# Reordering the head of a fused attention and gMLP kernel: q of the first block ahead of its k, loads in 128-row pieces, one store moved forward

## Chip, cores, metric

One core of one Trainium2 chip. The metric is device time in microseconds (us) of one execution. All runs in this document are at granted clock 0.997 to 1.0. The profiled span is about 1.7 us shorter than the time of the same execution.

## The reference, cut to what matters

```python
x  = A_x                                  # 1 x 2048 x 512, bf16
xn = layernorm(x)
# A: 32 heads of 16, a window of 8 keys two apart
q, k, v = split(xn @ wqkv);  o = softmax(q . k[gathered]) . v[gathered];  A = o @ wo
# B: gMLP
z = gelu(xn @ w_in);  z1, z2 = z[:, :688], layernorm(z[:, 688:])
B = (z1 * (w_sp @ z2 + b_sp)) @ w_out
return x + A + B
```

The change concerns the first 25 us only (normalise, transpose, q and k projections of the first two of four token blocks) and one store at the end.

## The kernel before: the parts that matter

A block is four tiles of 128 tokens. A tile is normalised on VectorE (`ln_stats`, `ln_apply`; the root on ScalarE), transposed into `xnT`, and multiplied with q's and k's weights on TensorE (PE). Block 0's tiles and the first two of block 1 are transposed on PE (`tr`) and copied out. All others go through a transposing DMA from SyncE (`tr_dma`). A call of `qk_part` with `m` 0 or 1 makes half of q, with 2 or 3 half of k; `b0, b1` are the tiles it covers.

```python
    def tr_dma(i):
        SP.dma_start_transpose(xnT[:, :, i * P:(i + 1) * P], xall[:, j, tb, :])
    ...
    load_wqk(SP, 0, 0, 2); load_wqk(SP, 0, 2, 4)       # q weights, 2 x 256 KB
    SP.dma_start(xall[:, 1, 0:2], xblk[1][:, 0:2])
    load_wqk(SP, 1)                                    # k weights, 512 KB
    ...
    warm_up(10)                    # PE work on a zero tile, 512 columns each
    ...
    for n in range(2, 4):
        ln_apply(i1[n])
        tr_dma(i1[n])              # tiles 2 and 3 of block 1: two transposing DMAs
    ...
    for c in range(3):
        qk_part(pqs[c], 1, c, 0, 2)        # block 1, first half
    pa3 = ps_aux.tile(...)
    qk_part(pa3, 1, 3, 0, 2)               # the `pa` group of the profile
    qk_copy(pa3, 1, 3, 0, 2)
    for c in range(3):
        qk_part(pqs[c], 1, c, 2, 4)        # block 1, second half: needs those two DMAs
        qk_copy(pqs[c], 1, c)
    ...
    for c in range(3): z matmuls ...       # "first z matmul" below (in the order list: z2.0)
```

Of the kernel before, what the change touches and what calls it, by code (L numbers as in the profile page):

```python
# [14 lines left out]
P = 128  # L15
S = 2048
D = 512
NT = S // P
TB = 4
TBS = 512  # L20
C = D // P
# [5 lines left out]
F = 1376  # L27
FH = 688
# [26 lines left out]
A35 A36 Oh0.1 Fe0.0 A37 Fe0.1 A38 G14 Fe0.2 Fe0.3 F0.2 F0.0 F0.1 s0.0 A39 s0.1 F0.3 A40 xr1 A41 Oh1.0 w13 A42  # L55
U10 Oh1.1 Fe1.0 U9 T8 Gi14 A43 Fe1.1 A44 T10 X13 A45 G11 s0.2 T9 A46 s0.3 F1.0 A47 A48 G13 F1.1 Gi11 s1.1 Xg13
U11 U12 Fe1.2 A49 T12 A50 A51 X14 A52 G15 Xg14 Fe1.3 U14 Gi13 F1.3 F1.2 A53 s1.2 T11 A54 T14 A55 O2 Gi15 s1.0
A56 U15 U13 T15 A57 Or2 xr2 Oh2.0 A58 A59 s1.3 Oh2.1 T13 Fe2.0 Fe2.1 xr3 F2.0 O3 Fe2.2 Fe2.3 F2.2 F2.1 s2.2
F2.3 s2.1 s2.3 Or3 Oh3.0 Oh3.1 F3.0 F3.1 s3.0 s3.1 s2.0 end
"""  # L60
NZ1 = 8
LASTCUT = 288
# [7 lines left out]
def kernel(  # L70
# [13 lines left out]
    V = nc.vector  # L84
    A = nc.scalar
    G = nc.gpsimd
    PE = nc.tensor
    SP = nc.sync
# [3 lines left out]
    xblk = x2.rearrange("(b j p) d -> j p b d", b=TB, j=4)  # L92
# [9 lines left out]
    xall = r_x[:, 0:4 * TB * D].rearrange("p (j b d) -> p j b d", j=4, b=TB)  # L102
    vp = r_x[:].rearrange("p (d t) -> p d t", d=DH)
    r_w = sb.tile([P, 8192], BF16, name="r_w")
    wqk = r_w[:, 0:4096].rearrange("p (s k f) -> p s k f", s=2, k=C)
# [30 lines left out]
    xnT = sb.tile([P, C, S], BF16, name="xnT")  # L136
    w_z2 = sb.tile([P, C, FH], BF16, name="w_z2")
# [27 lines left out]
    def load_x0(E, tb, h):  # L165
        E.dma_start(xall[:, 0, tb, 256 * h:256 * h + 256], x2[tb * TBS:tb * TBS + P, 256 * h:256 * h + 256])

    def load_wqk(E, s, k0=0, k1=C):
        E.dma_start(wqk[:, s, k0:k1],
                    A_wqkv[:, s * D:(s + 1) * D].rearrange("(k p) f -> p k f", p=P)[:, k0:k1])  # L170

    for tb in range(2):
        load_x0(SP, tb, 0)
        load_x0(A, tb, 1)
    for tb in range(2, TB):
        A.dma_start(xall[:, 0, tb], xblk[0][:, tb])
    load_wqk(SP, 0, 0, 2)
    load_wqk(SP, 0, 2, 4)
    SP.dma_start(xall[:, 1, 0:2], xblk[1][:, 0:2])
    load_wqk(SP, 1)  # L180
    SP.dma_start(xall[:, 1, 2:4], xblk[1][:, 2:4])
    for j in range(2, 4):
        SP.dma_start(xall[:, j], xblk[j])
    SP.dma_start(w_z2[:], B_w_in[:, FH:F].rearrange("(k p) f -> p k f", p=P))


    V.memset(warm[:, 0:P], 0.0)
# [17 lines left out]
    def ln_stats(i, parts=1):  # L205
        j, tb = i % 4, i // 4
        w = D // parts
        for h in range(parts):
            V.bn_stats(stats[:, i, 6 * h:6 * h + 6], xall[:, j, tb, w * h:w * h + w])  # L209
        V.bn_aggr(mv[:, i, :], stats[:, i, 0:6 * parts])  # L210

    def ln_root(sl):
        A.activation(rstd[:, sl], mv[:, sl, 1], ACT.Abs_reciprocal_sqrt, bias=eps_t[:])

    def ln_apply(i):
        j, tb = i % 4, i // 4
        V.tensor_scalar(xall[:, j, tb, :], xall[:, j, tb, :], mv[:, i, 0:1], rstd[:, i:i + 1],
                        ALU.subtract, ALU.mult)

    def tr(i):  # L220
        j, tb = i % 4, i // 4
        pt = ps_aux.tile([P, C, P], BF16, name="pt", tag="aux")
        for c in range(C):
            PE.transpose(pt[:, c, :], xall[:, j, tb, c * P:(c + 1) * P], ident[:])  # L224
        return pt

    def tr_copy(i, pt, c0=0, c1=C):
        A.copy(xnT[:, c0:c1, i * P:(i + 1) * P], pt[:, c0:c1, :])

    def tr_dma(i):  # L230
        j, tb = i % 4, i // 4
        SP.dma_start_transpose(xnT[:, :, i * P:(i + 1) * P], xall[:, j, tb, :])
# [57 lines left out]
    def qk_part(pq, j, m, b0, b1, ccs=(0, 1), p0=None, kcs=range(C)):  # L290
        sd, c0 = m // 2, 2 * (m % 2)
        p0 = b0 if p0 is None else p0
        xv = xnT[:].rearrange("p k (b j t) -> p k b j t", b=TB, j=4)
        for cc in ccs:
            for kc in kcs:
                PE.matmul(pq[:, cc, p0 * P:(p0 + b1 - b0) * P], wqk[:, sd, kc, c0 + cc:D:C],  # L296
                          xv[:, kc, b0:b1, j, :], start=(kc == 0), stop=(kc == C - 1))

    def qk_copy(pq, j, m, b0=0, b1=TB, p0=None):
        sd, c0 = m // 2, 2 * (m % 2)  # L300
        p0 = b0 if p0 is None else p0
        if sd == 0:
            dst = qs[:, j, c0:c0 + 2, b0 * P:b1 * P].rearrange("p c (b t) -> p c b t", b=b1 - b0)
        else:
            dst = ks[:, c0:c0 + 2, HALO:HALO + S].rearrange("p c (b j t) -> p c b j t", b=TB, j=4)[:, :, b0:b1, j, :]
        cast = A.copy(dst, pq[:, :, p0 * P:(p0 + b1 - b0) * P].rearrange("p c (b t) -> p c b t", b=b1 - b0))  # L306
        if sd == 1:
            for i in k_reads[j]:
                tc.declare_no_dep(cast.ins, i, reason="other token columns of the same rows")
            k_casts[j].append(cast.ins)  # L310

    def qk_tile():
        return ps_mm.tile([P, 2, TBS], F32, name="pq", tag="mm")
# [224 lines left out]
    def blk(j):  # L538
        return [4 * tb + j for tb in range(TB)]

    def col(i):
        return slice(i, i + 1)

    def blk_cols(j):
        return slice(j, NT, 4)
# [6 lines left out]
    t0, i1 = blk(0), blk(1)  # L552
    i2, i3 = blk(2), blk(3)
# [4 lines left out]
    for n in range(2):  # L558
        ln_apply(t0[n])
    tr_copy(t0[0], tr(t0[0]))  # L560
    pt1 = tr(t0[1])
    tr_copy(t0[1], pt1, 0, 2)
    tr_copy(t0[1], pt1, 2, 4)
    warm_up(1)
    warm_up(1, 2)
# [5 lines left out]
    pqs = [qk_tile() for _ in range(3)]  # L571
    qk_part(pqs[0], 0, 0, 0, 2, kcs=range(2))
    qk_part(pqs[0], 0, 0, 0, 2, kcs=range(2, 4))
    tr_copy(t0[2], tr(t0[2]))
    qk_part(pqs[1], 0, 1, 0, 2, (0,))
    tr_copy(t0[3], tr(t0[3]))
    qk_part(pqs[1], 0, 1, 0, 2, (1,))
    qk_part(pqs[2], 0, 2, 0, 2)
    for n in range(2):
        ln_stats(i1[n])  # L580
    ln_root(slice(1, 8, 4))
    ln_stats(i1[2])
    ln_apply(i1[0])
    ln_apply(i1[1])
    ln_stats(i1[3])
    for n in range(2):
        qk_part(pqs[n], 0, n, 2, 4)
        qk_copy(pqs[n], 0, n)
    ln_root(slice(9, 16, 4))
    ln_stats(i2[0])  # L590
    for n in range(2, 4):
        ln_apply(i1[n])
        tr_dma(i1[n])
    qk_part(pqs[2], 0, 2, 2, 4, (0,))
    tr_copy(i1[0], tr(i1[0]))
    qk_part(pqs[2], 0, 2, 2, 4, (1,))
    tr_copy(i1[1], tr(i1[1]))
    qk_copy(pqs[2], 0, 2)
    pq3 = qk_tile()
    qk_part(pq3, 0, 3, 0, 4)  # L600
    qk_copy(pq3, 0, 3)
    for n in range(1, 4):
        ln_stats(i2[n])
    ln_root(blk_cols(2))
    ln_stats(i3[0])
    for i in i2:
        ln_apply(i)
        tr_dma(i)
    for n in range(1, 4):
        ln_stats(i3[n])  # L610
    pqs = [qk_tile() for _ in range(3)]
    for c in range(3):
# [76 lines left out]
```

## Time and profile before

| | before |
|---|---|
| time, median of the 6 runs beside the changed kernel | 203.12 us (202.78 to 203.41) |
| span of the profiled run | 201.6 us |
| PE's last matmul ends, last instruction to span end | 196.30, 5.3 us |
| first z matmul | 22.90 |

PE's timeline before, 18 to 23 us (start, length, what, count):

```profile
18.37 1.04 PE L296 MATMUL pa<-xnT,r_w 128*128 128x256 bf16 x8
19.25 3.66 PE L296 MATMUL pq<-xnT,r_w 128*128 128x256 bf16 x32
22.74 1.48 PE L238 MATMUL pz<-w_z,xnT 128*128 128x344 bf16 x9
```

The second line is block 1's second half. It follows the `pa` group without a bracket, that is without a wait. ("The chain" is the profile's list of the work that ended last, followed back piece by piece to what released it. The timeline puts a start about 0.16 us ahead of where the chain puts the same group when there is no wait: the chain has 18.54, 19.41 and 22.90.) Its input, the second transposing DMA's result, had come in time. SyncE's part of it, and a view of these DMAs with the time from issue to landing, in the kernel before:

```profile
14.63 10.39 SPq L232 DMA_TRANSPOSE xnT<-r_x  x7
DMA to landing us min/median/max: 2.4/2.5/3.0
```

The second one was issued at 16.04; its last packet was done by 17.99 (table below) and it landed at 18.44, so there was about 1 us of slack to 19.41.

### The profile page before, as it was taken

How to read it: one execution, taken by the hardware profiler on the slowest of the kernel's cores; microseconds unless marked ns; L12 is line 12 of the kernel's file. 1: busy time of each engine (PE TensorE's matmuls, PEld its weight loads, DVE VectorE, ACT ScalarE, POOL GpSimd, SP SyncE). 2: the span in 40 equal slices, each digit the busy share in tenths (PEclk: the TensorE clock that was granted, in tenths of full speed). 3: DMA queues.
4: the chain of work that ended last, by engine and by line, in shares of the span. 5: the costliest groups of instructions: out<-in, count | busy, mean ns of one | idle time of the engine just before them, and what ended most of it. 6: DMA issues, size and time to landing. Idle time of an engine off the chain costs nothing.

```text
span 201.6 us, 4025 instructions
## 1 busy us (share of the span) xinstructions
PE 196.2 (97%) x1667; PEld 124.7 (62%) x1667; DVE 184.4 (91%) x247; ACT 103.7 (51%) x172; POOL 18.3 (9%) x14
## 2 busy tenths in 40 slices
PE   7799999999999999999999999999999999999993
PEld 2589855665566666666656666666544646664562
DVE  5879699999989999999979999999999999999604
ACT  3565988899999996363341523808402230331400
POOL 3000000799500000000000000000000000000000
PEclk9999999999999999999999999999999999999999
DMA  5983549850000085544285999199920299215753
GB/s 151 337 279 74 90 98 273 177 111 0 3 0 3 0 134 109 162 92 104 62 150 135 247 255 166 34 227 169 224 65 0 87 222 142 73 42 129 205 177 130
DMA packets 66306, 25.91 MB, mean 129 GB/s; under 512 B 56240, under 2 KB 66032, under 8 KB 66032
## 3 DMA queue, kind: packets, MB, share of 16 engines
q1 hardware_dynamic: 65568, 25.19, 55.9%
q10 hardware_dynamic: 720, 0.47, 0.7%
q8 instruction: 13, 0.21, 0.4%
q14 instruction: 5, 0.04, 0.1%
HBM read 10.13 MB, written 2.10 MB: 61 GB/s over the span
## 4 chain that ended last, share of the span: by engine, by line
PE 92%; DMA 4%; DVE 1%; issue 0%; SPq 0%
PE pg L439 37%; PE pz L238 19%; PE pq L296 13%; PE pv L400 7%; PE po L522 7%; PE po L492 6%; DMA r_w<-in_A_wqkv_dram 3%; DMA r_x<-in_A_x_dram 1%; PE pa L522 1%; PE pl L350 1%; DVE r_pr L510 1%; PE po L501 1%; PE pb L492 1%; PE pa L296 0%; PE pt L224 0%
## 5 line engine op out<-in xcount | busy, mean ns | idle before, releaser
L439 PE MATMUL pg<-z,r_qk 128*128 128x344 bf16 x448 | 66.8, 309 | 0.0
L439 PEld LDWEIGHTS <-r_qk 128*128 128x128 bf16 x448 | 43.7, 98 | 22.0 <-issue 0.4
L414 DVE TENSOR_TENSOR r_pr<-r_x,r_w 128x2048 bf16<-128x2048 bf16 x32 | 38.4, 1219 | 1.3 <-PE pl L350 1.0
L238 PE MATMUL pz<-w_z,xnT 128*128 128x344 bf16 x256 | 39.3, 309 | 0.0
L418 DVE TENSOR_TENSOR r_pr<-r_pr 128x2048 bf16<-128x2048 bf16 x28 | 33.9, 1218 | 0.4
L238 PEld LDWEIGHTS <-xnT 128*128 128x128 bf16 x256 | 24.9, 98 | 13.2 <-issue 0.4
L445 ACT ACTIVATE gs<-pg,b_col 128x688 bf16<-128x688 f32 x16 | 13.2, 833 | 35.7 <-PE pg L439 26.4
L296 PE MATMUL pq<-xnT,r_w 128*128 128x256 bf16 (+1 forms) x176 | 28.7, 317 | 1.1 <-DMA r_w<-in_A_wqkv_dram 0.7
L330 DVE TENSOR_TENSOR r_pr<-r_qk 128x2048 bf16<-128x2048 bf16 x24 | 27.9, 1222 | 0.7 <-ACT r_qk L306 0.5
L296 PEld LDWEIGHTS <-r_w 128*128 128x128 bf16 x184 | 20.1, 114 | 8.8 <-issue 1.0
L631 POOL CAST b_col<-b 128x16 f32<-128x16 bf16 x1 | 16.2, 16244 | 34.1 <-DMA b<-in_B_b_sp_dram 34.1
L306 ACT CAST r_qk<-pq 128x1024 bf16<-128x1024 f32 (+1 forms) x16 | 15.4, 989 | 4.3 <-PE pq L296 4.1
L505 ACT CAST r_qk<-po 128x512 bf16<-128x512 f32 x10 | 5.5, 587 | 22.7 <-PE po L522 22.7
L287 ACT ACTIVATE r_uz<-pz 128x688 bf16<-128x688 f32 x16 | 11.7, 739 | 6.3 <-PE pz L238 6.2
L492 PE MATMUL po<-r_lg,r_pr 32*128 32x512 bf16 x192 | 14.5, 375 | 0.0
L400 PE MATMUL pv<-xnT,r_w 128*32 128x512 bf16 x256 | 14.2, 379 | 0.0
L522 PEld LDWEIGHTS <-r_uz 128*128 128x128 bf16 x85 | 8.0, 98 | 9.4 <-issue 1.1
L339 DVE TENSOR_TENSOR r_pr<-r_pr 128x4096 bf16<-128x4096 bf16 x6 | 13.7, 2288 | 0.0
L522 PE MATMUL po<-r_w,r_uz 128*128 128x512 bf16 x60 | 13.6, 380 | 0.0
L209 DVE BATCH_NORM_STATS2 stats<-r_x 128x6 f32<-128x512 bf16 (+1 forms) x18 | 10.9, 615 | 2.1 <-DMA r_x<-in_A_x_dram 2.1
L262 ACT ACTIVATE junk<-z 128x688 bf16<-128x688 bf16 x16 | 12.4, 773 | 0.1
L256 ACT ACTIVATE z<-pz 128x688 bf16<-128x688 f32 x16 | 11.8, 739 | 1.2 <-PE pz L238 1.2
(78 smaller groups left out, 184.6 us busy)
## 6 DMA issues: line engine op xcount, KB each, us to landing
r_lg<-in_A_wo_dram SPq DMA_DIRECT2D x8, 256.0 KB, 4.0
out_dram<-r_qk SPq DMA_DIRECT2D x12, 128.0 KB, 3.0
w_z<-in_B_w_in_dram SPq DMA_DIRECT2D x2, 688.0 KB, 6.8
r_w<-in_A_wqkv_dram SPq DMA_DIRECT2D x2, 512.0 KB, 5.3
r_x<-in_A_x_dram SPq DMA_DIRECT2D x2, 512.0 KB
r_qk<-in_A_x_dram SPq DMA_DIRECT2D x8, 128.0 KB, 2.5
r_w<-in_B_w_out_dram SPq DMA_DIRECT2D x1, 640.0 KB, 5.3
r_w<-in_A_wqkv_dram SPq DMA_DIRECT2D x2, 256.0 KB, 4.6
```

The costliest lines, as they stand in the source:

```text
L238: PE.matmul(pz[:, hh, 0:FHALF], xnT[:, kc, i * P:(i + 1) * P], wz[:, kc, hh * FHALF:(hh + 1) * FHALF], start=(kc == 0), stop=(kc == C - 1))
L296: PE.matmul(pq[:, cc, p0 * P:(p0 + b1 - b0) * P], wqk[:, sd, kc, c0 + cc:D:C], xv[:, kc, b0:b1, j, :], start=(kc == 0), stop=(kc == C - 1))
L306: cast = A.copy(dst, pq[:, :, p0 * P:(p0 + b1 - b0) * P].rearrange("p c (b t) -> p c b t", b=b1 - b0))
L330: prod = V.tensor_tensor(pr[g % 3][:, c].rearrange("p w b t -> p b w t"), q3.unsqueeze(2).broadcast_to([P, TB, 4, P]), k4, ALU.mult)
L339: V.tensor_tensor(pr[g % 3][:, 0:2], pr[g % 3][:, 0:2], pr[g % 3][:, 2:4], ALU.add)
L400: PE.matmul(pv[32 * tb:32 * tb + 32, dd, :], wv[:, kc, 2 * d2 + dd, :], xnT[:, kc, tb * TBS:(tb + 1) * TBS], start=(kc == 0), stop=(kc == ...
L414: V.tensor_tensor(pw_t[n], vp[:, :, off:off + P], a_sb[:, slot_w(w), ts].unsqueeze(1).broadcast_to([P, DH, P]), ALU.mult)
L418: V.tensor_tensor(pw_t[n] if dst is None else dst, pw_t[n], pw_t[m], ALU.add)
L439: PE.matmul(pg[:, hh, 0:FHALF], wsp[n][:, k, :], z2[:, k, hh * FHALF:(hh + 1) * FHALF], start=(k == 0), stop=(k == NT - 1))
L492: PE.matmul(pc, op[32 * tb:32 * tb + 32, d, o * P:(o + 1) * P], wo_r[32 * tb:32 * tb + 32, d, cs], start=(d == 8), stop=False, tile_positi ...
L522: PE.matmul(pc, uT[:, o % 2, m, tb * P:(tb + 1) * P], wout[:, m, cs], start=False, stop=(m == MCH - 3))
L631: G.tensor_copy(b_col[:], b16[:])
```

## The change

Intent: PE's wait for k's weights goes, because q of all four tiles of block 0 is done first; loads become 128 KB pieces in the order in which they are needed; roots are taken tile by tile so that normalisation does not wait for a pair; half of a PSUM copy moves to VectorE. The store that stood among the last ones is issued first of its group.

```diff
-F2.2 F2.1 s2.2 F2.3 s2.1 s2.3 ... s3.1 s2.0 end
+F2.2 F2.1 s2.0 s2.2 F2.3 s2.1 s2.3 ... s3.1 end
...
-    def load_wqk(E, s, k0=0, k1=C):
-        E.dma_start(wqk[:, s, k0:k1], ...)
+    def load_wqk(E, s):
+        for kc in range(C):
+            E.dma_start(wqk[:, s, kc], A_wqkv[kc * P:(kc + 1) * P, s * D:(s + 1) * D])
+    def load_x(E, j, b0, b1):            # one DMA of 128 rows per tile
...
-    for j in range(2, 4):
-        SP.dma_start(xall[:, j], xblk[j])
-    SP.dma_start(w_z2[:], ...)
+    load_x(SP, 2, 0, 4)
+    for kc in range(C):
+        SP.dma_start(w_z2[:, kc], ...)
...
+    def tr_copy_v(i, pt, c0, c1):        # the copy out of PSUM on VectorE
...
+    qk_part(pqs[1], 0, 1, 0, 2, (0,))
     tr_copy(t0[2], tr(t0[2]))
-    qk_part(pqs[1], 0, 1, 0, 2, (0,))
-    tr_copy(t0[3], tr(t0[3]))
-    qk_part(pqs[1], 0, 1, 0, 2, (1,))
-    qk_part(pqs[2], 0, 2, 0, 2)          # k, tiles 0 and 1: waits for k's weights
...
+    tr_copy_v(t0[3], pt3, 0, 2)
+    tr_copy(t0[3], pt3, 2, 4)
+    qk_part(pqs[0], 0, 0, 2, 4, kcs=range(2))    # q, tiles 2 and 3
+    qk_part(pqs[0], 0, 0, 2, 4, kcs=range(2, 4))
+    qk_part(pqs[1], 0, 1, 2, 4)
...
+    qk_part(pqs[2], 0, 2, 0, 4)          # k: 8 matmuls of 512 columns, were 16 of 256
...
     for n in range(2, 4):
         ln_apply(i1[n])
         tr_dma(i1[n])
+    load_x(SP, 3, 0, 4)                  # x of block 3 only here
```

More of the change, by code (lines that the diff above doesn't have):

```diff
@@ L57 @@
 U11 U12 Fe1.2 A49 T12 A50 A51 X14 A52 G15 Xg14 Fe1.3 U14 Gi13 F1.3 F1.2 A53 s1.2 T11 A54 T14 A55 O2 Gi15 s1.0
-A56 U15 U13 T15 A57 Or2 xr2 Oh2.0 A58 A59 s1.3 Oh2.1 T13 Fe2.0 Fe2.1 xr3 F2.0 O3 Fe2.2 Fe2.3 F2.2 F2.1 s2.2
-F2.3 s2.1 s2.3 Or3 Oh3.0 Oh3.1 F3.0 F3.1 s3.0 s3.1 s2.0 end
+A56 U15 U13 T15 A57 Or2 xr2 Oh2.0 A58 A59 s1.3 Oh2.1 T13 Fe2.0 Fe2.1 xr3 F2.0 O3 Fe2.2 Fe2.3 F2.2 F2.1 s2.0
+s2.2 F2.3 s2.1 s2.3 Or3 Oh3.0 Oh3.1 F3.0 F3.1 s3.0 s3.1 end
 """
@@ L166, in load_x0 @@
         E.dma_start(xall[:, 0, tb, 256 * h:256 * h + 256], x2[tb * TBS:tb * TBS + P, 256 * h:256 * h + 256])
-    def load_wqk(E, s, k0=0, k1=C):
-        E.dma_start(wqk[:, s, k0:k1],
-                    A_wqkv[:, s * D:(s + 1) * D].rearrange("(k p) f -> p k f", p=P)[:, k0:k1])
+    def load_wqk(E, s):
+        for kc in range(C):
+            E.dma_start(wqk[:, s, kc], A_wqkv[kc * P:(kc + 1) * P, s * D:(s + 1) * D])
+    def load_x(E, j, b0, b1):
+        for tb in range(b0, b1):
+            E.dma_start(xall[:, j, tb], xblk[j][:, tb])
     for tb in range(2):
@@ L174 @@
         load_x0(A, tb, 1)
-    for tb in range(2, TB):
-        A.dma_start(xall[:, 0, tb], xblk[0][:, tb])
-    load_wqk(SP, 0, 0, 2)
-    load_wqk(SP, 0, 2, 4)
-    SP.dma_start(xall[:, 1, 0:2], xblk[1][:, 0:2])
+    load_x(A, 0, 2, 4)
+    load_wqk(SP, 0)
+    load_x(SP, 1, 0, 2)
     load_wqk(SP, 1)
-    SP.dma_start(xall[:, 1, 2:4], xblk[1][:, 2:4])
-    for j in range(2, 4):
-        SP.dma_start(xall[:, j], xblk[j])
-    SP.dma_start(w_z2[:], B_w_in[:, FH:F].rearrange("(k p) f -> p k f", p=P))
+    load_x(SP, 1, 2, 4)
+    load_x(SP, 2, 0, 4)
+    for kc in range(C):
+        SP.dma_start(w_z2[:, kc], B_w_in[kc * P:(kc + 1) * P, FH:F])
     V.memset(warm[:, 0:P], 0.0)
@@ L228, in tr_copy @@
         A.copy(xnT[:, c0:c1, i * P:(i + 1) * P], pt[:, c0:c1, :])
+    def tr_copy_v(i, pt, c0, c1):
+        V.tensor_copy(xnT[:, c0:c1, i * P:(i + 1) * P], pt[:, c0:c1, :])
     def tr_dma(i):
@@ L573 @@
     qk_part(pqs[0], 0, 0, 0, 2, kcs=range(2, 4))
+    qk_part(pqs[1], 0, 1, 0, 2, (0,))
     tr_copy(t0[2], tr(t0[2]))
-    qk_part(pqs[1], 0, 1, 0, 2, (0,))
-    tr_copy(t0[3], tr(t0[3]))
-    qk_part(pqs[1], 0, 1, 0, 2, (1,))
-    qk_part(pqs[2], 0, 2, 0, 2)
-    for n in range(2):
-        ln_stats(i1[n])
-    ln_root(slice(1, 8, 4))
-    ln_stats(i1[2])
+    qk_part(pqs[1], 0, 1, 0, 2, (1,), kcs=range(2))
+    pt3 = tr(t0[3])
+    qk_part(pqs[1], 0, 1, 0, 2, (1,), kcs=range(2, 4))
+    tr_copy_v(t0[3], pt3, 0, 2)
[3 more added lines that the diff above has]
+    qk_part(pqs[1], 0, 1, 2, 4)
+    ln_stats(i1[0])
+    ln_root(col(i1[0]))
+    ln_stats(i1[1])
+    ln_root(col(i1[1]))
+    qk_copy(pqs[0], 0, 0)
     ln_apply(i1[0])
     ln_apply(i1[1])
-    ln_stats(i1[3])
-    for n in range(2):
-        qk_part(pqs[n], 0, n, 2, 4)
-        qk_copy(pqs[n], 0, n)
-    ln_root(slice(9, 16, 4))
-    ln_stats(i2[0])
+    qk_copy(pqs[1], 0, 1)
+    qk_part(pqs[2], 0, 2, 0, 4)
+    for n in range(2, 4):
+        ln_stats(i1[n])
+        ln_root(col(i1[n]))
     for n in range(2, 4):
@@ L593 @@
         tr_dma(i1[n])
-    qk_part(pqs[2], 0, 2, 2, 4, (0,))
+    load_x(SP, 3, 0, 4)
     tr_copy(i1[0], tr(i1[0]))
-    qk_part(pqs[2], 0, 2, 2, 4, (1,))
+    pq3 = qk_tile()
+    qk_part(pq3, 0, 3, 0, 4, (0,))
     tr_copy(i1[1], tr(i1[1]))
+    qk_part(pq3, 0, 3, 0, 4, (1,))
     qk_copy(pqs[2], 0, 2)
-    pq3 = qk_tile()
-    qk_part(pq3, 0, 3, 0, 4)
     qk_copy(pq3, 0, 3)
-    for n in range(1, 4):
+    for n in range(4):
         ln_stats(i2[n])
-    ln_root(blk_cols(2))
-    ln_stats(i3[0])
+    ln_root(slice(2, 7, 4))
+    ln_root(slice(10, 15, 4))
     for i in i2:
@@ L608 @@
         tr_dma(i)
-    for n in range(1, 4):
+    for n in range(4):
         ln_stats(i3[n])
```

## The prediction

> **What bounds the kernel now.** I read the page's first and fourth parts first. The second block is the chain of waits, in order of time, at its head.
>
> ```profile
> PE 196.2 (97%) x1667; PEld 124.7 (62%) x1667; DVE 184.4 (91%) x247; ACT 103.7 (51%) x172; POOL 18.3 (9%) x14
> PE 92%; DMA 4%; DVE 1%; issue 0%; SPq 0%
> ```
>
> ```profile
> 3.46 6.56 DMA r_w<-in_A_wqkv_dram
> 10.01 0.05 issue
> 10.06 3.25 PE pq L296 x28
> ```
>
> TensorE (PE) is busy for 97% of the span, but 97% is not the argument: the chain is. From 10.06 us the chain of the end consists of PE pieces only, without a break, until the last eviction at 196.3. The list of PE's waits from 22 us on is empty. So an instruction moved on another engine after 10.06 is worth something only if PE can be made to start its unbroken run earlier. What precedes that run is one transfer, the 512 KB of the k weights (issued at 3.46, landed 6.56 us later). The next view is PE's own timeline from 6 to 11 us (start, length, what, and in brackets the idle time before it):
>
> ```profile
> 6.74 1.03 PE L296 MATMUL pq<-xnT,r_w 128*128 128x256 bf16 x8 [0.40 <-ACT xnT L228]
> 7.91 0.40 PE L224 MATMUL pt<-ident,r_x 128*128 128x128 bf16 x4
> 8.14 0.60 PE L296 MATMUL pq<-xnT,r_w 128*128 128x256 bf16 x4
> 8.58 0.39 PE L224 MATMUL pt<-ident,r_x 128*128 128x128 bf16 x4
> 8.80 0.60 PE L296 MATMUL pq<-xnT,r_w 128*128 128x256 bf16 x4
> 10.06 3.25 PE L296 MATMUL pq<-xnT,r_w 128*128 128x256 bf16 x28 [0.65 <-DMA r_w<-in_A_wqkv_dram]
> ```
>
> The lengths overlap, so starts are what counts. Four matmuls of 256 columns need 4 x 0.109 = 0.44 us (later in the run, where PE never waits, 32 of them take 3.49 us in the chain, 0.109 each). Those that start at 8.80 have left the array's input free at 9.24, and the next starts at 10.06: a hole of 0.82 us, of which the view counts 0.65. What it waits for is k's weights; the q matmuls of the tiles 2 and 3, which need no k weights, stand behind it in program order.
>
> [...](3.49/32 = 0.109; eight of 512 columns in 1.73 us, 0.216 each). So turning 16 matmuls of 256 columns into 8 of 512 saves no PE time worth the name. [...]issues of 64, 128, 256 and 512 KB alike take 0.37 to 0.51 us here, and landing comes 2 to 6.6 us after. So cutting a load in four multiplies the issue time by four. [...]In the trace the engines move 341 to 357 GB/s from 7 to 14 us with the large loads; whether 128 KB loads reach that, nothing here shows yet.
>
> **The change part by part.**
>
> (a) *Order on PE.* The q matmuls of tiles 2 and 3 (16 of 256 columns, 1.74 us) move ahead of all k matmuls. Starting from 6.74: eight matmuls to 7.61, four to 8.05, the transposes of tile 2 (four, start to start 0.055 us) to 8.27, two matmuls to 8.49, transposes of tile 3 to 8.71, two matmuls to 8.93. The next group needs the transposed copies of tiles 2 and 3. ScalarE's copy of tile 2 starts at about 8.34 as before, 0.6 us, so 9.0; the new VectorE half copy of tile 3 starts at about 8.77 (its engine is free: the normalisation ends at 8.33) and takes some 0.3 us by estimate from ScalarE's 0.38 for a half; ScalarE's other half ends at 9.4. So PE goes on at about 9.2, with a hole of 0.25 in place of 0.82, and runs 16 matmuls to 10.93. k's weights are wanted at 10.93 (first quarter) to 11.6 (fourth) instead of 9.24. The state that PE had at 10.06 is reached at about 9.2: **0.86 us gained**.
>
> (b) *Loads of 128 KB.* The built order shows that each load waits for the one eight before it; that held before too, but with fewer, larger loads. Now k's weights are loads 13 to 16 and wait for x tiles and q weights that land at about 5 to 6.5. SyncE: 0.47 us each, the fourth quarter is issued at about 7 (before: whole at 3.46), and lands, with at most 1 MB outstanding at 340 GB/s (3 us), at 9.5 to 10. That is no earlier than the 10.01 of before, but PE now wants it at 11.6. So this wait should be gone with 1 to 2 us to spare. x of block 1, tiles 2 and 3, should land at 10 to 11 (before 10.80), wanted by VectorE at 11.5. Block 2 and the z weights follow by 13 to 15.5, wanted at 14.2 and 22. x of block 3 is issued only after the first transposing DMAs, at 16.3, lands by 20.5, wanted from 19.1 on, tile by tile.
>
> (c) *Roots tile by tile, and the rest of the head.* A pair's root becomes two of 0.29 us: 0.3 us more on ScalarE. VectorE: statistics and applications as before plus 0.3 for the copy. My schedule: statistics of block 1's first two tiles end at 10.75, applications at 11.5, next statistics at 13.1, applications at 14.2 (before 14.92). ScalarE: two q evictions at 11.05 to 13.0, roots to 13.5, transposed copies to 14.7, two k evictions to 16.7. PE finishes block 0 at 14.83 (before: 14.19 + 1.73 = 15.92) and block 1's third group waits about 0.15 for the eviction at 16.7; it starts the `pa` group at 17.6 against 18.54. So **0.9 us** is still there, and at the first z matmul (22.90 before, 22.0 now) too. VectorE starts its products 0.65 us earlier (24.0 instead of 24.69): its idle of 1.6 before the last normalisations shrinks.
>
> (d) *The store.* The tail in order of time:
>
> ```profile
> 198.03 0.42 SPq L517 DMA_DIRECT2D out_dram<-r_qk  x1
> 198.50 0.39 DVE L510 TENSOR_TENSOR r_pr<-pb,r_pr 128x224 bf16<-128x224 f32 x1
> 198.54 0.89 SPq L517 DMA_DIRECT2D out_dram<-r_pr  x2
> ```
>
> The store from r_qk at 198.03 is ready since about 191 and stands among the last ones. The final store can be issued when its addition ends at 198.89; it starts at 199.07, after its neighbour. Without the store between, the neighbour goes at 198.1 and the last at about 198.95: **0.1 us gained**. It costs 0.4 us of an idle queue earlier.
>
> The sum: 0.86 to 0.95 at the head, 0.1 at the end, about 1.0; I take 0.1 off for what is lost on the way. 203.12 - 0.9 = 202.2.
>
> **The rivals.**
> - *VectorE becomes the bound.* It is busy 91%, and gains only 0.65 in my schedule. The last additions of products end at 188.8 and PE reads them from 189.91: 1.1 us of slack; the second logits group at 48.7 comes 0.3 after its sums. If VectorE's gain rules, the total gain is 0.65 + 0.1: 202.4. For it: slack at 48.7 is small. Against: VectorE itself waits for PE at places (1.0 us for `pl`).
> - *Small loads starve the head.* If issue and the eight-deep limit hold loads to under 280 GB/s (128 KB per 0.47 us) with waits on top, block 1's x or k's last quarter comes 1 us late, ScalarE and PE wait for it in turn, and the gain goes: 203 or a bit more. For it: the rate is below the 341 of before. Against: all of it has about 1 us to spare, x of block 1 least.
> - *ScalarE becomes the link at 13 to 17 us:* it has roots, copies and four evictions in a row, and PE waits for freed PSUM tiles. Each 0.1 us of lateness is passed on; a loss of 0.3 gives 202.5.
> - *All holes vanish* (also the 0.25 at 9 us and the start before 6.74, because x lands earlier): the gain is 1.3: 201.8.
>
> **Range and chances.** The holes before 10.06 that the change can touch sum to little over 1 us, which is 0.5%, and its losses can hardly exceed that, so a move of 2% either way would need something unseen. Range 201.6 to 203.0; faster by over 2% 0.01, within 2% 0.98, slower by over 2% 0.01.
>
> **What would show it.** Right: PE's first k matmul of block 0 (eight of 512 columns) at about 10.9 with no wait for the weights, the first z matmul at about 22.0, no PE wait after it, PE's end 0.85 earlier, the last store right behind its addition. Wrong: a PE wait for the weight transfer or for ScalarE's evictions between 11 and 17 of over 0.3 us; VectorE waiting for block 1's x past 11.5; the first product no earlier than 24.69; or a PE wait for VectorE at 48 or 189.9.

Cuts are marked in it: what it said of the hardware that no trace or run of this case shows is taken out. The sum stays 0.86 to 0.95 at the head and 0.1 at the end, about 1.0, less 0.1 on the way, so 203.12 - 0.9 = 202.2.

Two of its statements on loads, as the traces show them. The wait for the load eight before is in the built program, and it is seen in both profiles: before, the ninth load is issued at 3.04, the first having landed at 3.03; after, the ninth at 2.96 (the first landed at 2.94) and the 24th at 10.27 (the 16th at 10.25). On issue time: k's weights took 0.47 us as one load of 512 KB and 0.43 to 0.44 each as four of 128 KB, so four times in sum is right there; the z weights took 2.21 us as one load of 688 KB and 0.33 to 0.43 each as four of 172 KB, so there it is not.

## The result and the profile after

| | before | after |
|---|---|---|
| median of 6 runs | 203.12 us (202.78 to 203.41) | 203.27 us (202.90 to 204.00) |
| ratio, 95% interval | 1 | 1.001 [0.9991, 1.0029] |
| profiled span | 201.6 | 201.2 |
| first z matmul | 22.90 | 22.84 |
| PE's last matmul ends | 196.30 | 196.25 |
| from there to the span's end | 5.3 | 4.95 |

Ratios in this document are the mean time of one kernel's fast runs over that of the other's of the same rounds, so not quite the ratio of the medians quoted. No change, then, and the prediction (202.2, range 201.6 to 203.0) was missed. The profiled run of the changed kernel was its fastest of six, so its span flatters it.

PE's timeline after, from 9 to 23 us (the bracket gives the idle time before and what ended it):

```profile
9.25 3.67 PE L301 MATMUL pq<-xnT,r_w 128*128 128x256 bf16 x24 [0.17 <-DVE xnT L233]
...
14.07 3.70 PE L301 MATMUL pq<-xnT,r_w 128*128 128x512 bf16 x28
17.61 1.04 PE L301 MATMUL pa<-xnT,r_w 128*128 128x256 bf16 x8
19.16 3.69 PE L301 MATMUL pq<-xnT,r_w 128*128 128x256 bf16 x32 [0.51 <-DMA xnT<-r_x]
```

Down to the `pa` group this is nearly the predicted schedule: the run starts at 9.25, there is no wait for k's weights, and `pa` starts at 17.61 where this view has 18.37 for the kernel before: 0.76 us gained. (The prediction's 17.6 looks like a hit, but it was set against the chain's 18.54, which promised 0.9.) Then block 1's second half, which had followed directly, waits for a transposing DMA. 17.61 + 8 x 0.109 = 18.48, and the group starts at 19.16: 0.68 us lost between starts (0.51 by the view's count). The chain of the end now runs through that DMA:

```profile
14.79 0.23 DVE stats L211
15.02 4.09 DMA xnT<-r_x
19.11 0.05 issue
19.16 3.69 PE pq L301 x32
```

The DMA took 4.09 us from issue to landing. The kernel before had 2.4 to 3.0 for DMAs of this kind. It was not issued late (15.02, before 16.04); it was slow. What lay beside it? Half-us windows of the changed kernel (columns: window; busy us of PE, PEld, DVE, ACT and POOL with counts; granted clock; DMA share; GB/s). The DMA share is packet time over the time of 16 engines, so a share far above 1 at a low rate is read here as packets that are outstanding and hardly move (by the packet records below, five of 256 bytes that started at 16.79 to 16.95 took 1.48 to 1.62 us each):

```profile
15.00:15.50 0.50, 0.50 (x7) 0.50 (x6) 0.47 (x2) 0.50 (x1) 0.00 (x0) 1.00 1.06 216
16.50:17.00 0.50, 0.50 (x7) 0.46 (x5) 0.47 (x2) 0.38 (x2) 0.00 (x0) 1.00 2.76 139
17.00:17.50 0.50, 0.50 (x8) 0.50 (x6) 0.50 (x3) 0.29 (x1) 0.00 (x0) 1.00 0.18 0
17.50:18.00 0.50, 0.50 (x7) 0.50 (x6) 0.50 (x2) 0.01 (x1) 0.00 (x0) 1.00 0.07 7
```

At 15 us the first transposing DMA moves with share 1.06. At 16.5 the second one has a share of 2.76, and then almost nothing moves for a microsecond. In the kernel before the second one had these windows:

```profile
17.00:17.50 0.50, 0.50 (x8) 0.50 (x5) 0.47 (x3) 0.13 (x1) 0.00 (x0) 1.00 0.50 104
17.50:18.00 0.50, 0.50 (x7) 0.50 (x6) 0.47 (x2) 0.17 (x1) 0.00 (x0) 1.00 0.78 158
```

Which queues had packets from 16 to 17 us in the changed kernel (queue and kind, packets, MB, share):

```profile
q1 hardware_dynamic: 500, 0.12, 163.3%
q8 instruction: 1, 0.02, 10.2%
```

Beside the transposing DMA there is a single other packet, of 16 KB, of kind "instruction". The page lists 13 such packets for a run, and PE has 3318 matmuls and weight loads, 255 per packet: by that count I take these for PE's own instruction blocks. The spacing agrees: from the start of the first such packet to that of the last, 12 packets on, the windows count 3081 matmuls and weight loads after and 3121 before, 257 and 260 per packet on average. That is an inference from counts; no record names the engine. In the kernel before the same window has no such packet; its packet lay at 14.00 to 14.95, ahead of the data of either transposing DMA.

Two other things differ in the trace after. VectorE waits for x of block 3, which is issued later than before:

```profile
19.89 0.69 DVE L211 BATCH_NORM_STATS2 stats<-r_x 128x6 f32<-128x512 bf16 x1 [1.44 <-DMA r_x<-in_A_x_dram]
...
24.85 2.35 DVE L335 TENSOR_TENSOR r_pr<-r_qk 128x2048 bf16<-128x2048 bf16 x2
```

Its products start at 24.85, where the kernel before had 24.69 and the prediction 24.0. And SyncE's last stores, whose old order the prediction shows, are now four in a row; the last issue ends at 199.19 instead of 199.43:

```profile
192.31 3.73 SPq L522 DMA_DIRECT2D out_dram<-r_qk  x4
196.99 2.20 SPq L522 DMA_DIRECT2D out_dram<-r_pr  x4
```

### The profile page after: what moved, and what is told of

It reads as the page before. It is cut to its first block, busy times and chain, and to the rows that moved or that the text cites. A ratio compares the mean times of both kernels' runs of the same rounds, so it can differ in the third digit from the quotient of the medians.

```text
span 201.2 us, 4028 instructions
## 1 busy us (share of the span) xinstructions
PE 196.0 (97%) x1659; PEld 123.7 (62%) x1659; DVE 184.5 (92%) x248; ACT 104.5 (52%) x175; POOL 17.4 (9%) x14
## 4 chain that ended last, share of the span: by engine, by line
PE 89%; DVE 5%; DMA 3%; ACT 1%; issue 1%
PE pg L444 37%; PE pz L243 19%; PE pq L301 10%; PE pv L405 7%; PE po L527 7%; PE po L497 6%; DVE stats L211 2%; DMA xnT<-r_x 2%; DMA r_x<-in_A_x_dram 1%; PE pa L527 1%; PE pl L355 1%; DVE r_pr L515 1%; PE po L506 1%; PE pb L497 1%; DVE r_x L219 1%; DVE mv L212 1%
## 5 line engine op out<-in xcount | busy, mean ns | idle before, releaser
L301 PEld LDWEIGHTS <-r_w 128*128 128x128 bf16 x176 | 19.2, 114 | 9.3 <-DMA xnT<-r_x 0.8
L641 POOL CAST b_col<-b 128x16 f32<-128x16 bf16 x1 | 15.4, 15356 | 35.1 <-DMA b<-in_B_b_sp_dram 35.1
```

The costliest lines, as they stand in the source:

```text
L301: PE.matmul(pq[:, cc, p0 * P:(p0 + b1 - b0) * P], wqk[:, sd, kc, c0 + cc:D:C], xv[:, kc, b0:b1, j, :], start=(kc == 0), stop=(kc == C - 1))
L641: G.tensor_copy(b_col[:], b16[:])
```

## The experiments

Theories, as the expectations name them. **A**: the late loads of x of block 3 collide with the transposing DMA or hold VectorE up. **B**: 128 KB loads drain more slowly than large ones, and the wait is their tail. **C**: the head does get faster, but a later wait takes it back. **D**: the fetch of PE's next instruction block, moved by the 16 fewer instructions, freezes the transposing DMA in flight. **E**: the fetch only happens to lie beside it. Twelve runs, all correct. None of them differs from the kernel before by 2%; what counts below is the intervals and the waits. The kernel before had medians of 203.01 (202.34 to 204.38), 203.06 (202.61 to 203.48) and 203.50 (202.34 to 204.66) in the three batches, 11 runs each. The batches ran on different chips, so medians are compared within a batch.

### First batch: parts of the change

**e1_x3_early**, the changed kernel with x of block 3 loaded early again:

```diff
     load_x(SP, 2, 0, 4)
+    load_x(SP, 3, 0, 4)
...
-    load_x(SP, 3, 0, 4)        # after the transposing DMAs
```

> The changed kernel with block 3's x loaded ahead of the z weights (as the kernel before has it) instead of between the transposing DMAs; nothing else differs. Theory A (the late x loads collide with the transposing DMAs of block 1, whose second landed 4.09 us after its issue instead of 2.5, and come late for VectorE): the second transpose lands by 18.0, PE's wait of 0.51 before 19.16 goes, PE reaches the first z matmul at 22.0 to 22.1 instead of 22.84, VectorE's 1.44 us wait for x goes and its products start at about 24.1 instead of 24.85, and the time is 0.6 to 0.9 us below the kernel before (ratio 0.9955 to 0.997). Theory B (transposes were slow because 128 KB loads drain more slowly and were still moving): with 512 KB more ahead of them they land even later, PE waits 0.5 or more, no gain (ratio 1.000 to 1.004). Theory C (head is gained but VectorE or a later wait takes it back): first z matmul at 22.0 but a new PE wait later, ratio 0.999 to 1.001.

Measured: 203.47 us (202.92 to 203.92), ratio 1.0008 [0.9974, 1.0043]. VectorE's wait for x is gone, but PE's wait has not shrunk, it has grown:

```profile
19.81 3.69 PE L302 MATMUL pq<-xnT,r_w 128*128 128x256 bf16 x32 [0.99 <-DMA xnT<-r_x]
```

The late x loads are not the cause: A falls. (In this run the last loads of the z weights also still moved, up to 16.76, beside the transposing DMAs; the instruction packet lay at 17.36 to 18.30, on the second one again.)

**e2_old_loads**, the changed kernel with the large loads of before (its `load_wqk` and its load list put back, everything else of after):

> The changed kernel with all loads as before (256, 512 and 688 KB, x of block 3 ahead of the z weights); keeps the new order of matmuls, the roots tile by tile and the moved store. Theory A: gains like e1, PE's first k matmul near 10.9, first z matmul at 22.0 to 22.2, ratio 0.9955 to 0.9975. If instead the small loads are needed for the new order (k weights at 10.06, x of block 1's last tiles at 10.80 are then too late), VectorE or PE waits 0.3 us or more between 9 and 14 and the ratio is 0.998 or more. Theory C: as in e1.

Measured: 203.13 us (202.80 to 203.29), ratio 0.9991 [0.9956, 1.0027]. The wait is still there, with all loads as before and no x load issued behind the transposing DMAs:

```profile
17.76 1.04 PE L299 MATMUL pa<-xnT,r_w 128*128 128x256 bf16 x8
19.43 3.69 PE L299 MATMUL pq<-xnT,r_w 128*128 128x256 bf16 x32 [0.63 <-DMA xnT<-r_x]
```

So B is not needed for it either: with the new order on PE the wait came in all three kernels so far, whatever the loads. The instruction packet lay at 16.92 to 17.80 here.

**e3_small_loads_only**, the kernel before with only the 128-row loads (x of block 3 early):

```diff
-    load_wqk(SP, 0, 0, 2)
-    ...
+    load_wqk(SP, 0)            # four pieces each, as in the changed kernel
+    ...
+    load_x(SP, 3, 0, 4)        # ahead of the z weights
```

> The kernel before with the loads in 128-row pieces, x of block 3 ahead of the z weights, nothing else changed. Theory A: issue-bound small loads cost nothing by themselves here, k weights land at 9.5 to 10 instead of 10.01, PE's run begins within 0.4 us of 10.06, ratio 0.998 to 1.001. Theory B: slower, ratio 1.001 to 1.004, a new PE wait for a transposing DMA before 19.4 or for the z weights at 22.9.

Measured: 203.75 us (202.89 to 204.81), ratio 1.0026 [0.9984, 1.0069]. In the profiled run (204.71, one of its two longest) the view shows no wait for k's weights, and PE loses more later:

```profile
8.60 4.08 PE L299 MATMUL pq<-xnT,r_w 128*128 128x256 bf16 x32
...
20.66 3.58 PE L299 MATMUL pq<-xnT,r_w 128*128 128x256 bf16 x31 [1.88 <-DMA xnT<-r_x]
```

Here the z weights' loads reach 18.30 and overlap the transposing DMAs. So loads that are still draining can produce the same wait (B in this kernel), but the changed kernel's are done by then. Why this kernel's instruction packet lies at 15.37, with the PE program of the kernel before (14.00), I could not settle.

**e4_store_only**, the kernel before with the store moved:

```diff
-F2.2 F2.1 s2.2 F2.3 s2.1 s2.3 ... s3.1 s2.0 end
+F2.2 F2.1 s2.0 s2.2 F2.3 s2.1 s2.3 ... s3.1 end
```

> The kernel before with only the one store moved. My prediction gave 0.1 us (ratio 0.9995); the profiled pair shows the stretch from PE's last big group to the end 0.35 us shorter in the changed kernel (4.95 against 5.30), which would be 0.9983. Rival: nothing, the end is set by the last store and its landing, ratio 0.9995 to 1.0005.

Measured: 202.62 us (202.12 to 202.81), ratio 0.9963 [0.993, 0.9997]. Its PE ends at 196.10 and its span at 201.1. From PE's end to the span's end is 5.0 us instead of 5.3. That distance is 5.26 to 5.31 in all kernels with the old place of the store and 4.9 to 5.0 in all with the new one: the store is worth about 0.3 us. The rest of this profiled run's lead is luck at the head:

```profile
9.85 3.25 PE L296 MATMUL pq<-xnT,r_w 128*128 128x256 bf16 x28 [0.15 <-DMA r_w<-in_A_wqkv_dram]
```

The wait for k's weights, 0.65 us in the profile of before that I predicted from, was 0.15 here with the same loads.

### What the packet records say

The trace also has each DMA packet's start and end. For the second transposing DMA, 512 packets of 256 bytes, the ends of the packets beside PE's instruction packet (kernels of the later batches are included):

```
kernel                instruction packet   packets of the second transposing DMA end       PE's wait
before                14.00 - 14.95        512 at 17.23 - 17.99                            none
after                 16.00 - 17.63        474 at 16.22 - 16.96, 38 at 17.66 - 18.45       0.51
after, again (y4)     16.24 - 17.83        473 at 16.39 - 17.13, 39 at 17.87 - 18.67       0.56
e2_old_loads          16.92 - 17.80        473 at 16.37 - 17.10, 39 at 17.83 - 18.67       0.63
e1_x3_early           17.36 - 18.30        468 at 17.00 - 17.66, 44 at 18.35 - 19.10       0.99
y1_pq2_halves         14.15 - 15.05        512 at 16.80 - 17.55                            none
x2_oldloads_page      13.45 - 14.55        512 at 16.27 - 17.03                            none
```

In the four runs with a late group, the last 38 to 44 packets do not end until the instruction packet has ended, and the very last comes 0.8 to 0.9 us after its end. The same distance stands in three later runs where the instruction packet lay on the first transposing DMA, which PE does not want so soon: x3, x4 and y3, last packet 0.83 to 0.84 us after it. In five profiles where neither DMA met such a packet or a load (before, e4, x2, y1, y2), each DMA's 512 packets pass in 0.76 to 0.88 us. For comparison, at the 341 GB/s that large plain loads moved side by side from 10 to 14 us in the kernel before, the same 128 KB would take 0.38 us by estimate; no run compares the two kinds directly.

The records also show how the late ones come. In the changed kernel 33 of the 38 start one after another from 17.61 on, some 0.025 us apart, as if they had stood in one queue behind the instruction packet. A sixteenth of 512 is 32, so this looks like the share of one of the 16 DMA engines; the records kept name no engine, so that part is inferred. Nor need it be an instruction packet: in x1 the last packet of the z weights ends at 15.91, and from then on 34 packets of the first transposing DMA start one after another, the last ending at 16.37; in e3 they start at 18.30, when the last z packet ends.

This picture is D's. It is still only a coincidence in time; the next runs move the packet.

### Second batch: moving the instruction packet

**x1_after_page**, the changed kernel with its warm-up cut into more and shorter matmuls, the same number of columns. That is 18 matmuls and 18 weight loads more, so if D holds the block boundary comes earlier in time:

```diff
-    warm_up(10)
+    warm_up(16, 2)
+    warm_up(8, 1)
...
-    warm_up(1)
-    warm_up(1, 2)
+    warm_up(6, 1)
```

> The changed kernel with its 12 warm-up matmuls cut into 30 smaller ones of the same number of columns: 36 more PE instructions before the real work, nothing else. Theory D (PE's 16 KB block of instructions, fetched by the DMA engines at 16.0 to 17.6 us in the changed kernel and at 14.0 to 14.95 in the kernel before, freezes the transposing DMA that is in flight): the fetch moves to before 14 us, the second transposing DMA of block 1 lands by 18.0 instead of 19.1, PE's wait before 19.16 goes, first z matmul at 22.0 to 22.2 instead of 22.84, VectorE's wait for block 3's x shrinks from 1.44 to under 0.5, ratio 0.995 to 0.997. Rival E (the transposing DMA is slow for some reason that instruction fetch only accompanies, such as the loads of x or being issued early): PE waits until about 19.1 as before, ratio 0.999 to 1.002.

Measured: 202.45 us (202.38 to 202.72), ratio 0.9975 [0.996, 0.9991], a little above the 0.995 to 0.997 expected. The packet lies at 13.72 to 14.60, the wait is gone, and so is VectorE's for block 3's x:

```profile
17.77 1.04 PE L301 MATMUL pa<-xnT,r_w 128*128 128x256 bf16 x8
18.64 3.66 PE L301 MATMUL pq<-xnT,r_w 128*128 128x256 bf16 x32
```

**x2_oldloads_page**, the same cut on e2_old_loads:

> The same cut of the warm-up in e2 (large loads as before, new order of matmuls, moved store). Theory D: the wait of 0.63 before 19.43 goes, first z matmul at 22.0 to 22.3, VectorE's products from about 24.1 to 24.3, ratio 0.995 to 0.997, as good as x1 or better. Rival E: wait stays, ratio 0.999 to 1.001.

Measured: 202.31 us (202.13 to 202.49), ratio 0.9965 [0.9951, 0.9979]; no wait, block 1's second half at 18.41, PE's end at 195.46.

**x4_before_page**, a control: the same cut on the kernel before.

> Control: the kernel before with the same cut of the warm-up. Its fetch at 14.0 already misses the transposing DMAs, so theory D expects no change on PE (run from 10.06, first z matmul 22.9, each within 0.3), ratio 0.998 to 1.002. If the cut of the warm-up itself helped or hurt [...], it would show here.

(The cut in it is a remark on why the warm-up might matter, which no trace here shows.)

Measured: 202.87 us (202.67 to 203.05), ratio 0.9993 [0.9979, 1.0008]. The cut alone does nothing to the median that these rounds can show. In the profile two expectations were missed: PE's run began at 9.57 and the first z matmul came at 22.42 in the chain, 0.5 us earlier than before, because k's weights happened to land at 9.52 instead of 10.01. The view shows no wait for them, though the chain still passes through that load and the starts leave a hole of 0.27:

```profile
8.86 3.96 PE L296 MATMUL pq<-xnT,r_w 128*128 128x256 bf16 x32
```

Nor was its packet at 14.0 or earlier: with 36 more PE instructions it lay at 14.63 to 15.72, on the first transposing DMA.

**x3_tiny_load**, the kernel before with one unused 16 KB load, meant to do to the second transposing DMA what the instruction packet does (the result is not affected):

```diff
     for n in range(1, 4):
         ln_stats(i2[n])
+        if n == 1:
+            V.memset(r_pr[0:1, 0:2], 0.0)
+            A.dma_start(r_pr[0:1, 0:8192], <first 16 KB of x>)
```

> The kernel before with one unused plain load of 16 KB into one partition, issued from ScalarE's queue at about 16 us, while block 1's transposing DMAs are in flight; it copies the size of an instruction block. Theory D, in its wider form (any plain transfer in flight freezes a transposing DMA until about 0.8 us after its own end): in the windows of half a microsecond between 16 and 19 the DMA share goes over 1 with little moved, as in the changed kernel (2.76 at 16.5 to 17.0), and block 1's second or block 2's first transposing DMA lands 0.5 to 1.5 us later than in the kernel before; PE waits before 19.4 if the delay is over 1.3. Rival E: DMA share stays at or below about 1.1 and landings are as before. Time within 0.3% either way.

Measured: 203.54 us (202.88 to 204.21), ratio 1.0026 [0.9998, 1.0054]. Part of the expectation was missed: the DMA share stayed at 1.09 or less, no packets of the second DMA hung for long, and PE had no wait. Its data, though, came only between 18.41 and 19.30, and the 16 KB packet ended at 18.46; between the two DMAs' data lies a gap of 0.9 us that the kernel before has as 0.6. The run is confounded: its instruction packet had moved too (15.58 to 16.68), and k's weights came late (a wait of 1.16). By itself it does not show that an ordinary 16 KB packet holds a transposing DMA back as well.

### Third batch: a second way to move it, and what each piece is worth

**y1_pq2_halves**, the changed kernel with 16 more PE instructions in another place, warm-up and loads untouched:

```diff
-    qk_part(pqs[2], 0, 2, 0, 4)
+    qk_part(pqs[2], 0, 2, 0, 2)
+    qk_part(pqs[2], 0, 2, 2, 4)
```

> The changed kernel with block 0's third group of q/k matmuls in two halves again (16 matmuls of 256 columns in place of 8 of 512): 16 more PE instructions ahead of block 1, the same PE time, warm-up and loads untouched. Theory D (the fetch of PE's next instruction block freezes the transposing DMAs in flight): the fetch moves from 16.0 us to some 14.3 to 15.2, ahead of the second transposing DMA's data; no PE wait for a transposing DMA at 19 us (0.51 in the changed kernel), first z matmul at 22.2 to 22.4 instead of 22.84, median 202.3 to 202.8. If the earlier cure came from the warm-up's own cut and not from the instruction count: wait of 0.4 to 0.6 stays, z at 22.8, median 203.0 to 203.4.

Measured: 202.29 us (202.09 to 202.39), ratio 0.9938 [0.9903, 0.9974] (the kernel before ran widely in these rounds). The packet went to 14.15 to 15.05, and:

```profile
17.78 1.04 PE L301 MATMUL pa<-xnT,r_w 128*128 128x256 bf16 x8
18.65 3.66 PE L301 MATMUL pq<-xnT,r_w 128*128 128x256 bf16 x32
22.15 2.06 PE L243 MATMUL pz<-w_z,xnT 128*128 128x344 bf16 x13
```

No wait; the z matmuls start 0.53 us earlier in the chain than in the changed kernel (22.31 against 22.84). The second transposing DMA in windows:

```profile
16.50:17.00 0.50, 0.50 (x6) 0.46 (x5) 0.50 (x2) 0.50 (x2) 0.00 (x0) 1.00 0.36 75
17.00:17.50 0.50, 0.50 (x7) 0.50 (x6) 0.47 (x3) 0.18 (x2) 0.00 (x0) 1.00 0.91 185
```

**y4_after_again**, the changed kernel unedited, same rounds:

> The changed kernel itself in these rounds, unedited. If its result holds: 202.9 to 203.4, ratio 0.999 to 1.002, a PE wait of 0.4 to 0.6 for a transposing DMA at 19 us and the fetch at 16.0. If the time of the fetch varies from run to run and the first profile was a stray: no such wait, and a median near 202.5.

Measured: 203.10 us (202.75 to 203.23), ratio 0.9978 [0.9945, 1.0011]. The wait is reproduced, with the packet at 16.24 to 17.83:

```profile
17.78 1.04 PE L301 MATMUL pa<-xnT,r_w 128*128 128x256 bf16 x8
19.38 3.69 PE L301 MATMUL pq<-xnT,r_w 128*128 128x256 bf16 x32 [0.56 <-DMA xnT<-r_x]
```

y1 and y4 start the `pa` group at the same 17.78. They differ by eight matmuls that PE does in the same time, and by 0.8 us in the median, with ranges that do not touch. The profiles explain 0.76 of it: PE ends at 195.71 against 196.47. (y4's wait cost 0.73 us between starts: 19.38 against 18.65.)

**y2_before_page_store**, the kernel before with the cut and the store, but the old order and copies:

> The kernel before with the cut warm-up and the moved store: everything of the best version but the new matmul order and the VectorE half copy. If the new order is worth its 0.4 to 0.9 us: 202.6 to 202.8, slower than the best version by 0.3 or more. If the store and the cut do it all: equal to the best version, 202.3 to 202.5. PE end to span end 4.9 to 5.0 in both cases.

Measured: 202.56 us (202.16 to 203.44), ratio 0.9961 [0.9924, 0.9997]. Its profiled run had the old hole in full:

```profile
10.25 3.25 PE L296 MATMUL pq<-xnT,r_w 128*128 128x256 bf16 x28 [0.95 <-DMA r_w<-in_A_wqkv_dram]
```

**y3_x2_again**, the best version repeated:

> The best version so far once more (the changed kernel with the loads of before and the cut warm-up): if its 202.31 holds: 202.1 to 202.5, ratio 0.996 to 0.997, no PE wait for DMA after 9 us, z at 21.9 to 22.1.

Measured: 202.18 us (202.04 to 202.78), ratio 0.9939 [0.9905, 0.9972]. Its packet came at 14.77 to 15.86, more than a microsecond later than in x2 with the identical program. It overlapped the first transposing DMA, and 39 of its packets ended only after it, the last at 16.69. The second was complete at 17.71, and PE, which wants it at 18.47, did not wait. So the packet's time varies from run to run, and a hold costs only where it falls on a transfer that is about to be wanted. The count of instructions is not all that sets this time: before, e4, e3 and x3 have one PE program, and their packets start at 14.00, 13.98, 15.37 and 15.58.

The new order is thus worth less in the median than the hole it removes in the one profile: y3 against y2 0.38 us, and x2 against x4 0.56 less the store's 0.3. Both are near the resolution of these rounds. The old hole is a matter of luck: by the view its wait was 0, 0.15, 0.65, 0.95 and 1.16 us in the five profiles with the old order and large loads (x4, e4, before, y2, x3); between starts it was 0.27, 0.31, 0.82, 1.11 and 1.32. The spread is in line with that: y1, x1 and x2 stay within 0.3 to 0.4 us over six runs each, the kernel before within 0.9 to 2.3 over eleven. It is not proof: y3 had one run 0.6 above its median, and x4, of the old order, stayed within 0.4.

## Why the prediction was wrong

- **(a) Order on PE, 0.86 us: right.** The run of q matmuls restarted at 9.25 (predicted 9.2), 0.81 us ahead of 10.06, with a view's wait of 0.17 after VectorE's half copy.
- **(b) Loads: right where it mattered.** k's weights were there before PE asked: the last quarter landed at 10.25, and PE, with sixteen q matmuls of 0.109 us to do from 9.25, wanted k's from about 11.0 by estimate. x of block 3 came as late as said, and VectorE waited 1.44 us for it, which the prediction had left unweighed. It cost nothing on PE: e1 removes that wait and is no faster.
- **(c) "So 0.9 us is still there, and at the first z matmul": this is the step that failed.** At `pa` 0.76 us was there (the schedule counted 0.109 us for every matmul; the first 28 after the wait at 10.06 take 3.25 us in the chain of before, 0.2 more than that). The schedule then assumed that block 1's second half follows at once. I had checked ScalarE's evictions, k's weights and x, but never the two transposing DMAs that feed this half. Their landing was assumed to move with the rest. Even at the old speed the margin was thin: in y1 the second landed at 18.05 and was wanted at 18.65. In the changed kernel it took 4.09 us and landed at 19.11. The wait of 0.68 us at 18.48 takes back nearly all of the 0.76: the first z matmul starts at 22.84 in place of 22.90.
- **What slowed it: shown as far as moving it goes.** Two independent edits that add PE instructions ahead of block 1, without adding PE time, move the instruction packet off the second transposing DMA, and the wait goes (x1, x2, y1); unedited it returns (y4). E would have had the wait stay. Removing the small loads (e2) or the late x loads (e1) does not remove it. That the held packets stand in one engine's queue behind the instruction packet fits the records (33 or 34 starting one by one at its end) but is inferred. What sets the packet's time besides the instruction count is open.
- **(d) The store, 0.1 us: right in kind, mis-sized.** It is about 0.3: from PE's end to the span's end it is 4.9 to 5.0 us in every kernel with it, 5.26 to 5.31 without. I counted the last store's issue (199.43 to 199.19 is 0.24, already more than 0.1); the rest is not resolved.
- **The rivals.** "VectorE becomes the bound" is refuted: from the first z matmul in the chain to PE's end it is 173.40 us before (22.90 to 196.30), 173.41 after (22.84 to 196.25), 173.40 in y1 (22.31 to 195.71) and 173.40 in y3 (22.13 to 195.53). A shift of the head, of up to 0.8 us here, reaches the end in full, which also disposes of C. "Small loads starve the head" named the right size (203 or a bit more) for a wrong reason, which is luck: with the large loads the result is the same (e2). "ScalarE becomes the link" and "all holes vanish" are not seen.
- **The sum.** With the one unforeseen wait taken away, and the rest of the change untouched, the time is 202.29 (y1), where 202.2 was predicted. That is in part luck: two errors cancel, a head worth 0.59 (first z matmul at 22.31 in place of 22.90) instead of 0.9 and a store worth 0.3 instead of 0.1, and the kernel before stood at 203.50 in those rounds. No rival had PE waiting for a transposing DMA.

## What to carry to other kernels

When a change starts a stretch of the bound engine earlier, go through every input of that stretch, not only those that the change touches: for each, when it lands now, what it is issued after, and how much slack is left once the engine comes earlier. Adding or removing instructions on PE also moved its instruction packet here (from 16.0 to 14.15 us with 16 more, y1), though it wandered by over a microsecond on its own (13.45 and 14.77 us in x2 and y3, one program); if a short wait appears on a DMA that nobody touched, look at which other queue had a packet in flight. And if a hole is made by a race between a load and an engine, read it in several runs before pricing its removal: one profile showed 0.65 us of a wait that lies between 0 and 1.2 in five.
